# Weights of w_down's last row loaded into TensorE ahead of the wait for the last transfer

## The chip, the core and the metric

The kernel runs on one core of a Trainium2 chip. The core has a matrix engine (TensorE, PE in the profile; its weight loads are listed as PEld), VectorE (DVE), ScalarE (ACT), GpSimd (POOL) and SyncE (SP). Each works through its own list of instructions, in order, and they wait for each other on semaphores. Transfers between device memory and on-chip memory (SBUF) run on 16 DMA engines, fed from queues; PSUM is the memory into which TensorE accumulates.

The metric is the device time of one execution in microseconds (us), as the median of several runs. Before the change it is 656.65 us in 3 runs (656.56 to 656.92).

## The reference

One decoding step of a transformer layer for one token: attention over a cache of 65,536 positions, then a gated feed-forward layer, each with a layer norm ahead and the input added behind.

```python
x = A_x                                          # 1 x 512, bfloat16
h = x + attention(layernorm(x), k_cache, v_cache, wq, wo)   # 32 query heads on 8 cached heads, head size 128
g = layernorm(h) @ w_gate                        # 512 x 1792
u = layernorm(h) @ w_up                          # 512 x 1792
h2 = h + (sigmoid(g) * u) @ w_down               # 1792 x 512
```

The two caches are 8 x 65536 x 128 bfloat16 each, 128 MB apiece; with the weights the kernel reads 282.33 MB.

## The kernel before, in words

The kernel is written out instruction by instruction, with no scheduler. `op` and `dma` append an instruction to one engine's list with the names that it waits for; `emit` turns the names into semaphore waits. A wait for several names stands ahead of its instruction, and everything behind it on that engine waits too. Loops over the cached heads stand in the lists of TensorE and VectorE.

All loads go through SyncE's queue, in one order written by hand: wq, then the K and V caches head by head into a ring in SBUF (`ring`), wo in two pieces, w_gate, w_up, and last w_down. w_down is read as 128 partitions x 14 rows of 512 (row `r` of partition `p` is row 14p + r of the matrix), and it comes in four pieces by rows, `WD_SPLIT`: 0 to 7, 8 to 10, 11 and 12, and 13 alone. Each piece has a semaphore of its own (`wd0` to `wd3`). The last piece, one row of 128 KB, is the last load of the kernel.

Per block of the K cache, VectorE transposes pieces (L531) and TensorE multiplies them by the query (L443, `mm_at`). There, one weight load serves four matmuls: `kept=True` makes a matmul without a load of its own (`ldweights=False`), which takes the weights that are in the array. V is multiplied by the transposed probabilities on the same line.

The tail, after the last V piece:
- the head's output goes through wo (L640, L650), the second layer norm follows (L400 to L414), and `hc`, the centred input, is ready;
- w_gate and w_up are multiplied by `hc` (L847), 448 columns in each of four column groups of the array, and L852 brings the residual into the bank `YB` of PSUM, where the output is collected;
- VectorE and ScalarE make the gated product `hh` (L859) and VectorE transposes it into `hhT` (L863), in two halves of seven rows (`HH`);
- for each of the 14 rows, four matmuls (L869) add `hhT`'s column times a quarter of w_down's row into `YB`. Quarter `g` works in column group `g` of the array (`tile_position=(0, 32*g)`), so that the four can run side by side. The weights are columns of `hhT`: 32 of them for even `g`, of which the last gives the row of the output that is read later, and one for odd `g`. The moving operand is 128 columns of w_down's row. The first matmul of each piece waits for that piece, the first of each half for `hhT`;
- the very last matmul (`r` = 13, `g` = 3) raises `y`. VectorE (L873) and ScalarE (L874) copy the two halves of the output from PSUM into `y_sb`, and two DMAs write them (L877).

`zcol` is a column of 128 zeros in SBUF, set once by GpSimd at the start.

Of the kernel before, what the change touches and what calls it, by code (L numbers as in the profile page):

```python
# [35 lines left out]
class Prog:  # L36
# [14 lines left out]
    def op(self, eng, fn, deps=(), name=None, to=None, times=1):  # L51
        assert name is None or name not in self.where, name
        self.ops[eng].append(dict(fn=fn, deps=[d for d in deps if d], name=name, dma=None, to=to, times=times, part=self.part.get(eng)))
        if name:
            self.where[name] = (eng, len(self.ops[eng]) - 1)
# [168 lines left out]
def bass_sequential_preLN__gqa_block_cached__glu_gated_glu__decode_kernel(  # L224
# [15 lines left out]
    NF = FF // 128  # L240
# [6 lines left out]
    with ExitStack() as es:  # L247
        def sb(name, shape, dt):
            return es.enter_context(nc.sbuf_tensor(name, shape, dt))
# [23 lines left out]
        zcol = sb("zcol", [128, 1], bf16)  # L273
# [29 lines left out]
        hhT = sb("hhT", [128, 32 + FG], bf16)  # L303
# [11 lines left out]
        def ps(bank, c0, c1, p0=0, p1=128):  # L315
            return PS[p0:p1, bank * 512 + c0: bank * 512 + c1]
# [5 lines left out]
        op, dma = P.op, P.dma  # L322
# [95 lines left out]
        n = 128 // XR  # L418
# [209 lines left out]
        YT, STB, GB, UB, YB, OT = 0, MISC, 2, 3, 5, (1, 1)  # L628
# [167 lines left out]
        for i in range(HKV + 1):  # L796
            loop, last = 0 < i < HKV, i == HKV
# [43 lines left out]
        wd_v = ring[:, AT["wd"] * CH:AT["wd"] * CH + NF * D].rearrange("p (r n) -> p r n", r=NF)  # L841
        for i, (nm, bank) in enumerate((("wg", GB), ("wu", UB))):
            at = W_AT[nm]
            for kt in range(4):
                for c in range(4):
# [3 lines left out]
                        rhs=ring[:, at + kt * FF + c * FG: at + kt * FF + (c + 1) * FG],  # L849
                        start=(kt == 0), stop=(kt == 3), tile_position=(0, 32 * c)),  # L850
# [6 lines left out]
        HH = ((0, 7), (7, NF))  # L857
        for i, (r0, r1) in enumerate(HH):
            op("dve", lambda e, r0=r0, r1=r1: e.tensor_tensor(  # L859
                hh[:, 32 * r0:32 * r1].rearrange("p (r q) -> p r q", q=32),  # L860
                ps(UB, 0, FG).rearrange("p (q r) -> p r q", r=NF)[:, r0:r1, :],
                sg2[:, :].rearrange("p (q r) -> p r q", r=NF)[:, r0:r1, :], ALU.mult), ["gu1", "sg2"], f"hh{i}")
            op("dve", lambda e, r0=r0, r1=r1: e.transpose(hhT[:, 32 + 32 * r0:32 + 32 * r1], hh[:, 32 * r0:32 * r1]), [f"hh{i}"], f"hhT{i}")  # L863
        for i, (r0, r1) in enumerate(WD_SPLIT):
            for r in range(r0, r1):
                for g in range(4):
                    last = r == NF - 1 and g == 3
                    m, c = (1, 32 * r + 32) if g % 2 else (32, 32 * r + 1)
                    op("pe", lambda e, r=r, g=g, m=m, c=c: e.matmul(  # L869
                        ps(YB, 0, 128, 32 * g, 32 * g + m), lhsT=hhT[:, c:c + m], rhs=wd_v[:, r, g * 128:(g + 1) * 128],  # L870
                        start=False, stop=(r == NF - 1), tile_position=(0, 32 * g), skip_group_check=True),
                       ((["hhTz", f"wd{i}"] if r == r0 else []) + [f"hhT{j}" for j, (h0, _) in enumerate(HH) if r == h0]) if g == 0 else (), "y" if last else None)
        op("dve", lambda e: e.tensor_copy(y_sb[0:33, :], ps(YB, 0, 128, 0, 33)), ["y"], "ysb0")  # L873
        op("act", lambda e: e.activation(y_sb[64:97, :], ps(YB, 0, 128, 64, 97), AF.Copy), ["y"], "ysb1")  # L874
        for i, eng in enumerate(("sp", "act")):
# [32 lines left out]
```

## Time and profile before

One execution was recorded by the profiler. Its span, from the first to the last instruction, is 655.2 us; the page gives no other time of that execution, and the median of the timed runs is 656.65 us.

| What | Before |
|---|---|
| median of 3 runs | 656.65 us |
| span of the profiled execution | 655.2 us |
| TensorE busy, matmuls | 398.7 us (61%), 2317 instructions |
| TensorE busy, weight loads | 66.8 us (10%), 1549 instructions |
| VectorE busy | 350.3 us (53%) |
| ScalarE busy | 43.1 us (7%) |
| read from device memory | 282.33 MB, 431 GB/s over the span |
| share of the span that the load queue's packets fill | 99.6% |

How to read such a profile: an engine's busy time is the union of its instructions' times, and it says nothing by itself about what sets the end. The chain of waits does: it goes back from the last instruction, at each step to what released it. Groups of instructions stand in one line each, with the line of the kernel, the engine, the operation, what it writes and reads, the shapes and the count, then the busy time in us, the mean of one in ns, the idle time of the engine just before them, and what ended it. "128\*32 128x128" at a matmul is a weight matrix of 128 rows and 32 columns, with 128 rows and 128 columns streamed through it. The ends of matmuls are modelled, and matmuls overlap each other, so the sum of their durations is more than the busy time. The granted clock is the share of TensorE's full clock in a stretch.

### The profile page before, as it was taken

The numbers are of one execution on the slowest core, as the hardware profiler recorded it, in microseconds if no ns is written. First come the engines' busy times: TensorE is split into PE (matmuls) and PEld (weight loads), VectorE is DVE, ScalarE is ACT, GpSimd is POOL, SyncE is SP. The second block draws the span as 40 slices with busy tenths as digits, with TensorE's granted clock in tenths as the row PEclk, the third lists the DMA queues.
The fourth block names the chain that finished last, engine by engine and source line by source line (L and its number), as shares of the span: only waits on it lengthen the run. The fifth ranks groups of instructions, "written<-read, shape, count | busy, mean of one in ns | idle before, by whom it ended". The sixth has DMA issues, their size and how long they took to land.

```text
span 655.2 us, 6177 instructions
## 1 busy us (share of the span) xinstructions
PE 398.7 (61%) x2317; PEld 66.8 (10%) x1549; DVE 350.3 (53%) x428; ACT 43.1 (7%) x114; POOL 3.7 (1%) x19
## 2 busy tenths in 40 slices
PE   2778672937548293674828467393845739285466
PEld 1100010110101000010100101010010101001122
DVE  3398853819266290935719184481917548092202
ACT  1100200020000200002000200002000020001001
POOL 1000000000000000000000000000000000000000
PEclk9799695977959687785978769595796958778656
DMA  9999999999999999999999999999999999999998
GB/s 396 436 436 460 436 396 448 448 448 408 424 448 448 444 392 444 448 448 420 412 448 448 448 408 424 448 448 440 392 448 448 448 412 420 448 448 444 412 404 356
DMA packets 6376, 282.33 MB, mean 431 GB/s; under 512 B 744, under 2 KB 872, under 8 KB 1256
## 3 DMA queue, kind: packets, MB, share of 16 engines
q1 hardware_dynamic: 6340, 282.33, 99.6%
q10 hardware_dynamic: 36, 0.00, 0.0%
HBM read 282.33 MB, written 0.00 MB: 431 GB/s over the span
## 4 chain that ended last, share of the span: by engine, by line
DMA 66%; DVE 30%; PE 2%; issue 1%; SPq 0%; PEldq 0%
DMA ring<-in_A_k_cache_dram 58%; DVE ktw L531 30%; DMA ring<-in_B_w_up_dram 4%; DMA ring<-in_A_v_cache_dram 4%; PE PS L443 2%; PE PS L869 0%; PE PS L847 0%; DVE hh L859 0%; DVE hhT L863 0%; SPq L368 0%; SPq L339 0%; DVE y_sb L873 0%; PEldq L171 0%
## 5 line engine op out<-in xcount | busy, mean ns | idle before, releaser
L531 DVE STREAM_TRANSPOSE ktw<-ring 128x1024 f32<-128x1024 f32 x256 | 291.6, 1209 | 164.6 <-DMA ring<-in_A_k_cache_dram 164.5
L443 PE MATMUL PS<-ktw 128*128 128x512 bf16 x1024 | 276.7, 419 | 162.7 <-DVE ktw L531 155.0
L443 PE MATMUL PS<-ring,PT_sb 128*32 x1024 | 85.7, 422 | 54.7 <-issue 46.3
L443 PEld LDWEIGHTS PS<-ktw 128*128 x256 | 26.3, 103 | 401.1 <-issue 233.3
L618 ACT ACTIVATE po_sb<-PS,rl 128x512 bf16<-128x512 f32 x8 | 5.5, 687 | 523.4 <-PE PS L443 523.4
L443 PEld LDWEIGHTS PS<-ring,PT_sb 128*32 x1024 | 20.7, 116 | 117.7 <-issue 116.4
L566 DVE TENSOR_REDUCE gmj<-PS 1x4 f32<-1x128 f32 x8 | 2.2, 279 | 53.9 <-PE PS L564 53.9
L538 DVE TENSOR_REDUCE M_sb<-PS 128x1 f32<-128x512 f32 x32 | 19.9, 683 | 19.3 <-PE PS L443 19.3
L577 ACT ACTIVATE P_sb<-PS,negmax 128x512 bf16<-128x512 f32 x32 | 21.5, 685 | 0.3
L587 DVE STREAM_TRANSPOSE PT_sb<-P_sb 128x512 bf16<-128x512 bf16 x32 | 19.9, 675 | 1.7 <-ACT P_sb L577 1.7
L443 PE MATMUL PS<-ktw,xz 128*8 x32 | 9.7, 476 | 6.0 <-DMA ktw<-in_A_wq_dram 6.0
L634 DVE TENSOR_TENSOR Lw<-O,blk_of 128x896 bf16<-128x896 bf16 (+1 forms) x2 | 1.4, 682 | 16.0 <-ACT O L624 16.0
L489 DVE STREAM_TRANSPOSE qt<-qh 32x512 bf16<-32x512 bf16 x1 | 0.7, 699 | 14.8 <-ACT qh L486 14.8
L571 PE MATMUL PS<-one_f,gmrep 1*128 1x1 f32 x16 | 4.6, 357 | 5.0 <-DVE gmrep L568 5.0
L564 PE MATMUL PS<-identf,gm 128*1 128x128 f32 x16 | 4.5, 379 | 5.1 <-issue 2.9
L643 DVE CAST O<-PS 128x28 bf16<-128x28 f32 (+1 forms) x2 | 0.3, 174 | 12.7 <-PE PS L640 12.7
L577 ACT ACTIVATION_READ_ACCUMULATOR P_sb<-PS,negmax 128x1 f32 x32 | 6.5, 203 | 0.0
L621 PE MATMUL PS<-sel_bf,po_sb 128*128 128x4 bf16 x32 | 2.1, 170 | 6.3 <-ACT po_sb L618 6.3
L504 ACT ACTIVATE PS<-zcol 128x512 f32<-128x512 bf16 x8 | 5.0, 623 | 0.0
L573 ACT ACTIVATE negmax<-PS 128x1 f32<-128x1 f32 x8 | 1.4, 171 | 54.0 <-PE PS L571 54.0
L592 PE MATMUL PS<-L_sb,lsel 128*128 128x4 f32 x16 | 2.5, 229 | 3.8 <-DVE PT_sb L587 3.8
L571 PEld LDWEIGHTS PS<-one_f,gmrep 1*128 1x128 f32 x16 | 4.0, 306 | 8.8 <-DVE gmrep L568 8.8
(89 smaller groups left out, 65.4 us busy)
## 6 DMA issues: line engine op xcount, KB each, us to landing
ring<-in_A_k_cache_dram SPq DMA_DIRECT2D x4, 4096.0 KB, 34.8
ring<-in_A_v_cache_dram SPq DMA_DIRECT2D x1, 5120.0 KB, 30.0
ktw<-in_A_wq_dram SPq DMA_DIRECT2D x1, 4096.0 KB, 12.2
ktw<-in_A_wo_dram SPq DMA_DIRECT2D x1, 3584.0 KB, 18.3
ring<-in_A_v_cache_dram SPq DMA_DIRECT2D x1, 3072.0 KB, 36.8
ring<-in_B_w_gate_dram SPq DMA_DIRECT2D x1, 1792.0 KB, 23.4
ring<-in_B_w_up_dram SPq DMA_DIRECT2D x1, 1792.0 KB, 27.2
ring<-in_B_w_down_dram SPq DMA_DIRECT2D x1, 1024.0 KB, 29.2
```

The lines of the kernel that those rows point to most:

```text
L443: return e.add_instruction(mybir.InstMatmult(name=nc.get_next_instruction_name(), engine=mybir.EngineType.PE, ins=[rhs, lhsT], outs=[e.low ...
L504: op("act", lambda e: e.activation(ps(PO, 0, 512), bass.AP(tensor=zcol, offset=0, ap=[[1, 128], [0, 512]]), AF.Copy), ["zcol"] if h == 0 e ...
L531: op("dve", lambda e, d=dst, sr=src: e.transpose(d, sr), deps, f"T{b}.{c}", to="T")
L538: op("dve", lambda e, u=u: e.tensor_reduce(M_sb[:, u % 4:u % 4 + 1], ps(u % NS, 0, 512), AX.X, ALU.max), [f"S{b}.{NC - NR + k}"], f"mx{u}" ...
L564: op("pe", lambda e: e.matmul(ps(MISC, 0, 128, 0, 1), lhsT=gm[:, :], rhs=identf[:, :], start=True, stop=True), [f"gm{h}"], f"gmT{h}", to="Q")
L566: op("dve", lambda e: e.tensor_reduce(gmj[:, :], ps(MISC, 0, 128, 0, 1).rearrange("p (i a c) -> p a i c", a=4, c=NC), AX.XY, ALU.max), [f" ...
L571: op("pe", lambda e: e.matmul(ps(MISC, 128, 129), lhsT=gmrep[0:1, :], rhs=one_f[0:1, 0:1], start=True, stop=True), [f"gmrep{h}"], f"neg{h}")
L577: op("act", lambda e, b=b: e.activation(P_sb[:, (b % 4) * 512:(b % 4 + 1) * 512], ps(b % NS, 0, 512), AF.Exp, bias=negmax[:, k:k + 1], sca ...
L587: op("dve", lambda e, b=b: e.transpose(PT_sb[:, (b % 4) * 512:(b % 4 + 1) * 512], P_sb[:, (b % 4) * 512:(b % 4 + 1) * 512]), [f"E{b}"], f" ...
L592: op("pe", lambda e: e.matmul(ps(MISC, 132, 136), lhsT=lsel[:, :], rhs=L_sb[:, :], start=True, stop=True), [f"PT{NR * h + NR - 1}"], f"l{h ...
L618: op("act", lambda e: e.activation(po_sb[:, :], ps(PO, 0, 512), AF.Copy, scale=rl[:, :]), [f"PV{h}.{NR - 1}", f"rl{h}"], f"po{h}", to="po")
L621: op("pe", lambda e, t=t: e.matmul(ps(OX, 0, 4), lhsT=po_sb[:, t * 128:(t + 1) * 128], rhs=sel_bf[:, 8 * t:8 * t + 8:2], start=(t == 0), s ...
```

## The change

For the last row only (`r` = 13), four more matmuls stand ahead of the wait for the last piece. Each loads the weights that the last row's real matmul in its column group needs and multiplies them by the single zero column `zcol`, which adds zeros to the first column of that group's output. The four real matmuls come behind the wait and load no weights. All matmuls of w_down now go through the helper `down`, which builds the instruction itself with the same operands, tile sizes and positions as before. The waits, their order, the transfers and the work of the other engines are the same; TensorE's list has four matmuls more and as many weight loads as before.

```diff
+        def down(e, r, g, ahead, kept):
+
+            m, c = (1, 32 * r + 32) if g % 2 else (32, 32 * r + 1)
+            n = 1 if ahead else 128
+            rhs = zcol[:, :] if ahead else wd_v[:, r, g * 128:(g + 1) * 128]
+            more = dict(ldweights=False) if kept else {}
+            return e.add_instruction(mybir.InstMatmult(
+                name=nc.get_next_instruction_name(), engine=mybir.EngineType.PE, ins=[e.lower_ap(rhs), e.lower_ap(hhT[:, c:c + m])],
+                outs=[e.lower_ap(ps(YB, 0, n, 32 * g, 32 * g + m))], start_tensor_calc=False, stop_tensor_calc=r == NF - 1 and not ahead,
+                tile_size=(128, 32), tile_position=(0, 32 * g), bass_skip_group_check=True, **more))
+
         for i, (r0, r1) in enumerate(WD_SPLIT):
             for r in range(r0, r1):
+                end = r == NF - 1
+                if end:
+                    for g in range(4):
+                        op("pe", lambda e, r=r, g=g: down(e, r, g, True, False))
                 for g in range(4):
-                    last = r == NF - 1 and g == 3
-                    m, c = (1, 32 * r + 32) if g % 2 else (32, 32 * r + 1)
-                    op("pe", lambda e, r=r, g=g, m=m, c=c: e.matmul(
-                        ps(YB, 0, 128, 32 * g, 32 * g + m), lhsT=hhT[:, c:c + m], rhs=wd_v[:, r, g * 128:(g + 1) * 128],
-                        start=False, stop=(r == NF - 1), tile_position=(0, 32 * g), skip_group_check=True),
-                       ((["hhTz", f"wd{i}"] if r == r0 else []) + [f"hhT{j}" for j, (h0, _) in enumerate(HH) if r == h0]) if g == 0 else (), "y" if last else None)
+                    op("pe", lambda e, r=r, g=g, end=end: down(e, r, g, False, end),
+                       ((["hhTz", f"wd{i}"] if r == r0 else []) + [f"hhT{j}" for j, (h0, _) in enumerate(HH) if r == h0]) if g == 0 else (),
+                       "y" if end and g == 3 else None)
```

## The prediction, made before the changed kernel ran

> **What bounds the kernel now.** I read the page's head, its chain of waits and its queue table first, then the chain in the last microseconds, the waits, and the last group of matmuls by form.
>
> ```profile
> span 655.2 us, 6177 instructions
> ...
> q1 hardware_dynamic: 6340, 282.33, 99.6%
> ...
> DMA 66%; DVE 30%; PE 2%; issue 1%; SPq 0%; PEldq 0%
> ```
>
> The load queue's packets fill 99.6% of the span. The kernel is a stream of 282 MB, and TensorE (PE) matters only behind the last pieces of that stream. So the whole change is worth what it does between the landing of the last transfer and the last instruction. Stretches of time (us, busy by engine, granted clock, DMA share) show how small that piece is:
>
> ```profile
> 616.00:648.80 32.80, 20.58 (x183) 6.54 (x179) 2.57 (x14) 1.31 (x3) 0.55 (x1) 0.65 0.99 426
> 648.80:653.25 4.45, 3.92 (x70) 2.07 (x70) 2.22 (x5) 0.18 (x1) 0.00 (x0) 0.50 0.85 342
> 653.25:655.25 2.00, 0.31 (x10) 0.11 (x4) 0.28 (x1) 0.27 (x1) 0.00 (x0) 0.50 0.00 1
> ```
>
> The last 2.00 us have no loads left; TensorE runs there at half its clock (0.50). The timeline of that piece (start, duration, engine, what, what ended the idle time before):
>
> ```profile
> 652.96 0.14 PEld L869 LDWEIGHTS PS<-ring,hhT 128*32 128x32 bf16 x8
> ...
> 653.26 0.11 PEld L869 LDWEIGHTS PS<-ring,hhT 128*32 128x32 bf16 x4 [0.16 <-DMA ring<-in_B_w_down_dram]
> 653.62 0.27 ACT L874 ACTIVATE y_sb<-PS 33x128 bf16<-33x128 f32 x1 [4.63 <-PE PS L869]
> 653.62 0.28 DVE L873 CAST y_sb<-PS 33x128 bf16<-33x128 f32 x1 [1.19 <-PE PS L869]
> ```
>
> The eight weight loads at 652.96 are the two rows of the third piece of w_down. The four at 653.26 are the last row; they stood 0.16 us for the last transfer, and that wait is the only one here that ends on data. Behind it stand four loads, four matmuls, and then VectorE and ScalarE from 653.62. From the wait's end to 653.62 there are 0.36 us, and this is all the time that the change can touch. The casts, the output DMA and its landing follow unchanged.
>
> **The change part by part.**
>
> *Weight loads taken from behind the wait.* Before, each of the last four matmuls has its load behind the wait. After, the loads stand with four one-column matmuls ahead of it, and the last four matmuls take the kept weights. What this buys is not the loads' busy time, because a matmul starts together with its load. The last four matmuls by form (count, busy us, mean ns), with the loads of that stretch below them:
>
> ```profile
> L869 PE MATMUL PS<-ring,hhT 128*32 128x128 bf16 x2 | 0.3, 288 | 0.0
> L869 PE MATMUL PS<-ring,hhT 128*1 128x128 bf16 x2 | 0.3, 264 | 0.0
> ...
> L869 PEld LDWEIGHTS PS<-ring,hhT 128*32 128x32 bf16 x2 | 0.1, 103 | 0.2 <-DMA ring<-in_B_w_down_dram 0.2
> L869 PEld LDWEIGHTS PS<-ring,hhT 128*1 128x1 bf16 x2 | 0.1, 79 | 0.0
> ```
>
> With 32 weight columns the load takes 103 ns and the matmul 288. With one column it is 79 and 264. So 24 ns more load make 24 ns more matmul, and the rest of the load is either inside the matmul's own latency or in its 264. The trace can tell which, because the score matmuls (L443) already use kept weights. At the start of a block at 0.50 clock, one matmul with its load and two with kept weights each wait for VectorE:
>
> ```profile
> 303.40:304.20 0.80, 0.61 (x1) 0.10 (x1) 0.80 (x2) 0.00 (x0) 0.00 (x0) 0.50 2.83 1229
> 304.20:306.80 2.60, 1.17 (x2) 0.00 (x0) 2.60 (x4) 0.00 (x0) 0.00 (x0) 0.50 0.99 429
> ...
> L443 PE MATMUL PS<-ktw 128*128 128x512 bf16 x1 | 0.6, 606 | 7.7 <-DVE ktw L531 7.7
> ...
> L443 PE MATMUL PS<-ktw 128*128 128x512 bf16 x2 | 1.2, 584 | 1.1 <-DVE ktw L531 1.1
> ```
>
> A load of 105 ns ahead of it (0.10 in the first stretch) costs the matmul 606 − 584 = 22 ns, not 105. The kept matmul streams 512 columns in 584 ns. The last row's stream 128, and 384 columns fewer at half clock are 320 ns, if half clock is 1.2 columns a nanosecond; this is an estimate from the spacing of the rounds below (128 columns in 105 ns). That gives 264, which is what the one-column matmuls already take with their load. So the load of one column is free today and that of 32 columns costs 24 ns. Of the four, the third has 32 columns and ends last. Taken: 24 ns. Ends of the price: 0 (if the end hangs on the fourth, one-column matmul, which also carries the semaphore) and 0.11 us (all the loads' busy time).
>
> In a sentence by itself: the Trainium skill (TensorE: Matmul & The Clock Gate, section LDWEIGHTS) puts a load at columns ÷ 1.2 ns, so 27 ns for 32 columns and 1 for one; the trace's 103 − 79 = 24 agrees with the difference and not with the whole, and the sum by it would be 3 ns more.
>
> *Fewer instructions behind the wait.* Eight become four. The eight loads at 652.96 begin and end within 0.14 us, of which one load alone has 0.10, so eight follow each other within 0.04 and four within 0.02; I take 6 ns, between 0 and 0.02.
>
> *Four zero matmuls and their loads, ahead of the wait.* Their cover is the 0.16 us for which the weight loader idles. The rounds of the first seven rows show how fast a row goes:
>
> ```profile
> 651.72 0.94 PE L869 MATMUL PS<-ring,hhT 128*32 128x128 bf16 x28 [0.45 <-DVE hhT L863]
> ...
> L869 PE MATMUL PS<-ring,hhT 128*1 128x128 bf16 x4 | 0.4, 311 | 0.0
> ```
>
> 28 matmuls are seven rounds of four, side by side in the array. The last one of them takes about 311 ns, and so a round follows another after (0.94 − 0.31) ÷ 6 = 0.105 us. The third piece's two rounds begin at 652.96 and have streamed by about 653.17. The zeros then stream one column each. For a matmul of one column the nearest row is the wo projection, sixteen of them one after another:
>
> ```profile
> 644.84 0.69 PE L650 MATMUL PS<-O,ktw 128*128 128x1 bf16 x16 [0.26 <-DVE O L643]
> ```
>
> 0.69 less one latency of about 0.17 is 0.52 ÷ 15 = 35 ns each, one behind another and at the full clock; half clock doubles that at most, to 70. Side by side the four need one such step, one behind another four. So the array is free again between 653.21 and 653.45, and I take 653.24, since the rows above run side by side. The wait ends at 653.26, so the zeros cost nothing, with a margin of some 0.02 to 0.05 us. If the cover is gone (the last transfer landing with the one before), the price is the same 0.04 to 0.28 us less what the loads save. The PSUM column into which they add receives zeros; no other engine waits on them, and no wait or DMA is added or moved.
>
> *Sum, against the profiled span.* 655.2 − 0.024 − 0.006 = 655.17. The median of the runs, 656.65, is 1.45 above the span (start and end, which the trace does not hold, and the spread of the runs, 656.56 to 656.92). So 656.65 − 0.03 = 656.62. With the ends: 0.13 faster (0.11 + 0.02) to 0.19 slower (zeros done at 653.45), 656.52 to 656.84. I count as no change what stays within 0.2%, 1.31 us, about what a measurement of this kernel can tell.
>
> **The rivals.**
>
> *The zeros come late* (+0.2 us, 656.85). If a weight load could not run beside a matmul of the third piece, the four loads would begin when that piece's last matmul ends, at 653.36:
>
> ```profile
> 652.76 0.60 PE L869 MATMUL PS<-ring,hhT 128*1 128x128 bf16 x12
> ```
>
> Then 0.10 for the load, about 0.04 for a zero's step and 0.264 for the last matmul end at 653.76, against 653.26 + 0.29 = 653.55 now. Against it: a load (103) and a matmul (311) one after another would make a round of 0.41, and the rows above show 0.105, so loads do run beside matmuls of the same rows. For it: the margin is only some hundredths.
> Beside it stands the Trainium skill (TensorE: Matmul & The Clock Gate, section Part 3: Packing small matmuls, "What overlaps and what doesn't"), where loads overlap only with matmuls of other row groups, and all four here use the same rows; the rounds of this trace speak against that.
>
> *The change saves nothing* (656.65). The end is set by the fourth matmul, 264 ns before and after.
>
> *Slower: PE lacks its code* (+0.7 to +4.7 us). PE's list is four instructions longer, right before the last wait. If these push the end of the list over the edge of the piece of code that PE holds, PE stands between the third piece's rows and the last wait until the next piece is there. It decides as soon as that takes over the 0.16 us of cover. The trace shows no such load, so it is bounded by small transfers, from issue to landing, of the input x and of the output, where SyncE waits for the landing:
>
> ```profile
> xs<-in_A_x_dram ACTq DMA_DIRECT2D x1, 1.0 KB, 4.9
> ...
> SPq L221 <- DMA out_dram<-y_sb: 0.9, 1, 0.9
> ```
>
> 0.9 − 0.16 gives 657.4, 4.9 − 0.16 gives 661.4. A read is nearer to the first row, so I take 660. Against it: from 640 us on, the waits name data or an engine for every stretch in which the matmul side of PE stood; "issue" stands only at the weight loader:
>
> ```profile
> PEld PS L443 <- issue: 1.7, 2, 0.9
> ...
> PEld PS L847 <- issue: 0.9, 4, 0.2
> PEld PS L869 <- DMA ring<-in_B_w_down_dram: 0.9, 2, 0.7
> ...
> PEld PS L852 <- issue: 0.8, 1, 0.8
> ```
>
> There the loader stood while the matmuls ahead were still streaming. A list that arrives in time today for the 70 matmuls and 70 loads after 648.80 should do so for four more.
> The Trainium skill (Runtime: NRT & Kernel Launch, section Instruction fetch mechanics) says that code comes in blocks of 256 instructions and that crossing an edge is mostly hidden, a taken branch not; no run here shows either.
>
> *Faster by more than 0.2%.* All the time from the last wait's end to the two casts is 0.36 us, so no mechanism of the change reaches 1.31. Only the same edge of code, moved to the better side, could do it, by 1.3 us or more; nothing shows that it costs that today.
>
> **How the numbers follow.** The forecast (−0.03) has 0.70, the zeros late 0.06, nothing saved 0.07: all three within 0.2%, 0.83 together. PE without its code has 0.13, of which 0.02 would stay within the bound, so slower is 0.11 and within 0.85. The moved edge has 0.04, which is faster. The range takes the ends of the sum (656.52 to 656.84), the spread of the runs around them (0.09 down, 0.27 up) and some of the slower case's lower end: 656.2 to 657.5. What it leaves out is mostly the slower case and the faster one.
>
> **What would show it right or wrong.** In the profile after, the four weight loads stand before the wait, and the last four matmuls start some 0.04 us after the last landing with about 264 ns each, all four alike. The casts start 0.33 us after the last wait's end instead of 0.36. The zeros begin before that wait's end, and PE idles for the last transfer still, by less than 0.16 us. The forecast is wrong if the last matmuls take more than 288 ns, if the zeros end behind the last landing, or if PE has an idle stretch in its tail with no releaser.

## The result, and the profile after

The changed kernel takes 660.25 us (median of 5 runs, 660.11 to 660.30), the kernel before 656.65 (656.47 to 657.41). The ratio is 1.0052, with a 95% interval of 1.0041 to 1.0063: slower by 3.6 us, where the forecast was 0.03 us faster.

Only 0.6 us of that are in the span of the profile, and the spans of the changed kernel's five runs (655.4 to 655.8 us) come near to the 655.2 of before. The page of the changed kernel, head and queue table:

```profile
span 655.8 us, 6181 instructions
...
q1 hardware_dynamic: 6340, 282.33, 99.6%
```

So the kernel's own instructions take about as long as before, and the loss lies outside the span. The profiled execution of the changed kernel has 660.3 − 655.8 = 4.5 us there, and its five runs have 4.5 to 4.8. The prediction had 1.45 us for the kernel before, which is a median less the span of another execution. In the 25 runs of the kernel before that were taken beside the first experiments, each with its own span, it is 1.3 to 1.4.

The tail itself did what the prediction said. Its timeline (start, duration, engine, what, and the idle time before):

```profile
653.08 0.88 PE L870 MATMUL PS<-ring,hhT 128*32 128x128 bf16 x24
653.62 0.18 PEld L870 LDWEIGHTS PS<-zcol,hhT 128*1 128x1 bf16 x4
653.73 0.24 PE L870 MATMUL PS<-zcol,hhT 128*1 128x1 bf16 x4
653.85 0.27 PE L870 MATMUL PS<-ring,hhT 128*32 128x128 bf16 x4
654.17 0.27 ACT L886 ACTIVATE y_sb<-PS 33x128 bf16<-33x128 f32 x1 [4.39 <-PE PS L870]
654.17 0.28 DVE L885 CAST y_sb<-PS 33x128 bf16<-33x128 f32 x1 [1.14 <-PE PS L870]
```

The first line holds the last matmuls of the rows ahead. The loads and zeros start ahead of 653.85, where the last four matmuls begin with no load behind them; from there to the casts it is 0.32 us, against 0.36 before. The trace also records when the last piece landed: at 653.81, 0.04 us ahead of the last four matmuls, as in the kernel before (653.22 and 653.26). So the zeros do not hold them up. From that landing to VectorE's cast it is 0.359 us, against 0.395 before. The four matmuls by form (mean ns after the bar):

```profile
L870 PE MATMUL PS<-ring,hhT 128*32 128x128 bf16 x2 | 0.3, 265 | 0.0
L870 PE MATMUL PS<-ring,hhT 128*1 128x128 bf16 x2 | 0.3, 264 | 0.0
```

288 has become 265, and the 264 of the one-column groups stayed.

The loss shows only in a view that goes past the span. The queues from 656 to 660 us (each digit is a slice of 0.1 us; then packets, MB and the share of 16 engines' time):

```profile
DMA  0000000000000000000600000000000000000000
GB/s 0 0 0 0 0 0 0 0 0 0 0 0 0 0 0 0 0 0 0 164 0 0 0 0 0 0 0 0 0 0 0 0 0 0 0 0 0 0 0 0
DMA packets 1, 0.02 MB, mean 4 GB/s; under 512 B 0, under 2 KB 0, under 8 KB 0
...
q8 instruction: 1, 0.02, 1.7%
```

One packet of the kind "instruction", 16384 bytes, starts in the slice at 657.9, 2.1 us after the kernel's last instruction. Its share is 1.7% of 16 engines over 4 us, which is about 1.1 us on one engine. These 2.1 and 1.1 us and the usual 1.3 to 1.4 add up to the 4.5 outside the span; what passes in the 2.1 us, no view shows. The kernel before has nothing of that kind in its span or behind it. Its queues from 653 us to the end:

```profile
DMA packets 8, 0.00 MB, mean 0 GB/s; under 512 B 8, under 2 KB 8, under 8 KB 8
...
q1 hardware_dynamic: 4, 0.00, 0.0%
q10 hardware_dynamic: 4, 0.00, 0.0%
```

### The profile page after: what moved, and what is told of

It is laid out like the page before. It is cut to its first block, busy times and chain, and to the rows that moved or that the text cites. A ratio compares the mean times of both kernels' runs of the same rounds, so it can differ in the third digit from the quotient of the medians.

```text
span 655.8 us, 6181 instructions
## 1 busy us (share of the span) xinstructions
PE 398.0 (61%) x2321; PEld 66.8 (10%) x1549; DVE 350.1 (53%) x428; ACT 43.1 (7%) x114; POOL 3.7 (1%) x19
## 4 chain that ended last, share of the span: by engine, by line
DMA 66%; DVE 30%; PE 3%; issue 1%; SPq 0%; PEldq 0%
DMA ring<-in_A_k_cache_dram 58%; DVE ktw L531 29%; DMA ring<-in_B_w_up_dram 4%; DMA ring<-in_A_v_cache_dram 4%; PE PS L443 2%; PE PS L870 0%; PE PS L847 0%; DVE hh L859 0%; DVE hhT L863 0%; SPq L368 0%; SPq L339 0%; DVE y_sb L885 0%; PEldq L171 0%
```

## The experiments

Two theories stood after that. C: PE's list, four instructions longer, pushes the instructions that close the program over the edge of a piece of code (the place where one piece ends and the next has to be there), and the next piece is fetched only when it is needed. T: the new form of the last row is itself what makes the end late. All times below are medians beside runs of the kernel before on the same chip.

**The same length, another place.** The kernel before, with four instructions that do nothing for the result (one load, three zero matmuls into an unused column) where PE waits for wq:

```diff
+        for i in range(3):
+            op("pe", lambda e, i=i: spare(e, i > 0), ["zcol"] if i == 0 else ())
```

`spare` multiplies `zcol` by itself; `kept`, its second argument, leaves out the load.

> The kernel before, with one more weight load and three one-column zero matmuls (four instructions) in PE's list near its head, where PE waits some 6 us for wq; the tail is as before. Theory C (PE's list has become four instructions too long; the instructions that close the program behind the kernel's last one pass the edge of a 16 KB piece of code, which is fetched only then): 660.2 us, span 655 to 656, and one instruction transfer of 16384 B some 2 us after the span's end. Theory T (the new form of the last row itself, zero matmuls and kept weights, makes the end of the program late): 656.6 us, no such transfer.

Measured: 660.10 us against 656.65, ratio 1.0053 (1.0036 to 1.0070), span 655.3. Its queues from 656 to 660 us:

```profile
DMA  0000000000000080000000000000000000000000
...
q8 instruction: 1, 0.02, 2.1%
```

The whole loss is there, and the transfer too, in the slice at 657.4, with a tail that is the old one. Theory T is refuted.

**The change, the old length.** The changed kernel, with w_up's rows in reverse order so that its first four matmuls keep w_gate's last weights:

```diff
+            kts = (3, 2, 1, 0) if i else (0, 1, 2, 3)
+            for k, kt in enumerate(kts):
...
+    more=dict(ldweights=False) if i and k == 0 else {}
```

> The changed kernel, with four weight loads saved elsewhere: w_up's rows are taken in the order 3, 2, 1, 0, and its first four matmuls keep the weights of w_gate's last four, which are the same. PE's list is then as long as before. Theory C: 656.6 us (0.03 to 0.1 below the kernel before), no instruction transfer after the span. Theory T: 660.2 us.

Measured: 656.58 us, ratio 0.9999 (0.9989 to 1.0008). From 656 to 660 us there is no transfer of any kind:

```profile
DMA packets 0, 0.00 MB, mean 0 GB/s; under 512 B 0, under 2 KB 0, under 8 KB 0
```

So the loss hangs on the length of PE's list and not on what the four instructions do.

**Another engine.** The kernel before with four memsets more on VectorE:

```diff
+        for i in range(4):
+            op("dve", lambda e, i=i: e.memset(scr[:, 40 + i:41 + i], 0.0))
```

> The kernel before, with four more one-column memsets in VectorE's list near its head, where it waits for x. Theory C, which ties the loss to PE's list of 483 instructions: 656.6 us, no instruction transfer after the span. A wider theory, that any longer program loses it: 660.2 us.

Measured: 656.66 us, ratio 1.000 (0.999 to 1.001). The time is as theory C has it, but the expectation of no transfer was wrong. The queues from 654 to 656 us (slices of 0.05 us):

```profile
DMA  0000090000000000000000000000000000000000
...
q8 instruction: 1, 0.02, 3.9%
```

A transfer of the same size starts in the slice at 654.25, 0.9 us before the span's end at 655.1, when the loads are over and the output is being written. It takes 3.9% of 16 x 2 us, 1.25 us, and costs nothing there. That the edge belongs to each engine's own list fits this, but the trace doesn't name the engine that asked, here or above: that the late transfer is PE's code rests on the runs in which only PE's list was changed. Why this one came so much earlier than PE's stays open.

**Where the edge lies.** Two more instructions (zeros and kept weights for the two 32-column groups alone) and three more (one load and two zero matmuls near the head of the kernel before):

```diff
-                    for g in range(4):
+                    for g in (0, 2):
...
-                    op("pe", lambda e, r=r, g=g, end=end: down(e, r, g, False, end),
+                    op("pe", lambda e, r=r, g=g, end=end: down(e, r, g, False, end and g % 2 == 0),
```

> The changed kernel, with the zero matmuls and kept weights for the two 32-column groups alone; the one-column groups load behind the wait as before. PE's list is two instructions longer than before instead of four. Theory C: 656.6 if the edge lies at three or four more, 660.2 if it lies at one or two more, and nothing between. Theory T: about half the loss, 658.4 us, if it goes by the count of zero or kept matmuls.

> The kernel before, with one weight load and two zero matmuls more near the head of PE's list: three instructions more. Theory C is a threshold between two more (656.6 us was not changed by more than the runs' spread) and four more (660.1): either 660.1 with an instruction transfer some 2 us after the span, or 656.6 with none; nothing between. If the loss grew with each instruction, it would be some 3 us x 3/4.

Two more: 657.02 us, ratio 1.0005 (0.9996 to 1.0015), and no instruction transfer; the total can't be told from no change. The time outside the span can: it is 1.5 to 1.7 us in all ten runs, against 1.3 to 1.4 in the 25 runs of the kernel before beside them and in the ten of the changed kernel in the old length. So some 0.3 us are lost behind the last instruction here already, where theory C had nothing between its two outcomes. The profile shows no transfer for it, and its cause is open.

In the tail of this kernel, the last matmuls begin at 653.16 and the casts at 653.43, 0.27 us:

```profile
653.16 0.23 PE L870 MATMUL PS<-ring,hhT 128*32 128x128 bf16 x4
653.16 0.08 PEld L870 LDWEIGHTS PS<-ring,hhT 128*1 128x1 bf16 x2
653.43 0.27 ACT L886 ACTIVATE y_sb<-PS 33x128 bf16<-33x128 f32 x1 [4.35 <-PE PS L870]
```

That stretch had the full clock (1.00), and so it is compared with the old tail at the full clock, in the kernel with four more at the head (653.39 to 653.69, 0.30). Counted from the recorded landing of the last piece to VectorE's cast, the old tail takes 337 ns there, this kernel 317, and the changed kernel in the old length, also at the full clock and with all four groups' weights kept, 308. So the 32-column groups bring 20 ns of the gain and the one-column groups 9.

Three more: 658.23 us, ratio 1.0023 (1.0008 to 1.0039), and neither of the two outcomes expected. The ten runs lie between 656.69 and 660.40: three up to 656.85, two at 657.2 to 657.4, and five from 659.1 up. At the edge itself the same program falls on either side, or between, by the run. The instruction transfer was there in the profiled run, after the span. Outside the span, four of the ten runs have the 1.6 to 1.7 us of two more, and the others 2.2 to 5.0. This is read as a transfer that sometimes comes in time; no short run of this kernel was profiled, and what decides it was not found.

**Far over the edge.** The changed kernel with 20 and with 56 instructions more at the head, to see whether the transfer moves with the edge:

```diff
+        for i in range(19):      # 55 in the other
+            op("pe", lambda e, i=i: spare(e, i > 0), ["zcol"] if i == 0 else ())
```

> The changed kernel with twenty instructions more near the head of PE's list (one weight load, nineteen zero matmuls), where PE waits for wq. Theory C1 (the missing piece of code is asked for when PE gets to its edge, and that edge moves forward through the closing instructions by as many as are added): the transfer starts earlier than the 2.2 us after the span that it has in the changed kernel, by 0.3 to 1 us, and the time is as much less: 659.2 to 660. Theory C2 (the request comes at a fixed point of the end, wherever the edge is): 660.2 again.

> The changed kernel with fifty-six instructions more near the head of PE's list. Theory C1: the edge now lies in or before the last matmuls instead of in the closing instructions, so the transfer starts before the output is written, near or ahead of 654 us, and runs beside the last work: 656.6 us, although the list is the longest of all; if the edge lies in the tail's matmuls and nothing fetches ahead, PE stands for 1 to 3 us inside the span instead (658 to 660, span 657 to 658). Theory C2: 660.2 us.

Measured: 657.76 us (1.0017, 1.0007 to 1.0026) and 658.03 (1.0020, 1.0011 to 1.0030), below the changed kernel with a longer list. Both theories on the place were wrong. The transfer did not come some tenths of a microsecond earlier, but early in the stream: at 101 us with 20 more, and at 94 us with 56 more. The kernel with 20 more, its queues from 100 to 103 us:

```profile
q1 hardware_dynamic: 16, 1.05, 81.7%
q8 instruction: 1, 0.02, 1.9%
```

1.9% of 16 x 3 us is 0.91 us on one DMA engine, beside the K and V loads. The 1.2 us that are lost now lie inside the span (656.5). The end of the stream shows how, in busy time by engine, clock, DMA share and GB/s; first the kernel before, then the one with 20 more:

```profile
652.00:653.00 1.00, 1.00 (x45) 0.77 (x40) 0.41 (x1) 0.00 (x0) 0.00 (x0) 0.50 0.62 221
653.00:654.00 1.00, 0.56 (x16) 0.21 (x12) 0.28 (x1) 0.27 (x1) 0.00 (x0) 0.50 0.00 0
```

```profile
652.00:653.00 1.00, 0.60 (x2) 0.30 (x2) 0.97 (x3) 0.00 (x0) 0.00 (x0) 0.50 0.70 256
653.00:654.00 1.00, 0.95 (x38) 0.88 (x42) 0.73 (x2) 0.00 (x0) 0.00 (x0) 0.50 0.07 26
```

Before, the loads end within the slice from 652. With 20 more, a share of 0.07 goes on through the next microsecond: 1/16 is 0.0625, so one DMA engine of the 16 is still working off its part, and the last pieces of w_down wait for it.

That this began with the code is in the trace's record of landings, sixteen for each load. In the kernel before, the last of the sixteen lands 0.08 to 0.16 us behind the fifteenth in every load. With 20 more it is up to 0.2 us in the loads that land by 89 us, and 1.3 to 1.4 in every later one, from 110 us to the last piece. One part stays late from the code transfer to the end. The trace doesn't name the DMA engines, so that it is the one that carried the code is the plain reading and not shown; nor is it shown why the 0.91 us became 1.3.

**The prefetch hint.** PE's list ends in a branch back that is never taken, with a prefetch hint at the list's start. The changed kernel without both, and with six instructions more at the head, so that its list is longer than that of the changed kernel:

```diff
-HINTED = ("pe", "dve", "act")
+HINTED = ("dve", "act")
...
+        for i in range(5):
+            op("pe", lambda e, i=i: spare(e, i > 0), ["zcol"] if i == 0 else ())
```

> The changed kernel without the never-taken backward branch and its prefetch hint in PE's list (four instructions of control less there), and six instructions more at the head, so that the list is one longer than in the changed kernel and over the edge too. Theory H (the hint holds back the fetch of the code that follows, so that it comes on demand): without it the next piece is fetched ahead, the transfer lies inside the span, and the time is 656.6 us or up to 1 us more for what the hint saved. If the hint has no part in it: 660.2 us with the transfer after the span.

> The changed kernel with two instructions more near the head of PE's list, the prefetch hint in place. Theory H (with the hint, the piece beyond the edge is not fetched until PE needs it, as long as the hinted branch itself lies before the edge): transfer some 2 us after the span, 660.2 us, span 655 to 656. If it was not the hint's absence but the greater length that moved the transfer to 101 us in the kernel without the hint (one instruction longer than the changed one): transfer near 101 us, 657.7 us, span 656.4.

> The changed kernel with ten instructions more near the head of PE's list, the hint in place. Between two more and twenty more, theory H has one switch, where the hinted branch passes the edge: either 660 us with the transfer after the span (perhaps a little earlier than 2.2 us behind it) or 657.7 us with it near 101 us. Nothing between.

Without the hint: 657.68 us (1.0015, 1.0005 to 1.0025), span 656.4, and the transfer stands in the queues from 100 to 103 us (1.9%), inside the span as theory H says; the time is 1.1 us above the kernel before, just over the 1 us that H allowed. With the hint and two instructions more than the change: 660.29 in two runs (1.0054, 1.0036 to 1.0072), span 655.7, and the transfer after the span:

```profile
DMA  0000000000000000600000000000000000000000
...
q8 instruction: 1, 0.02, 1.7%
```

So at about the same length, the hint keeps the code from being fetched at 101 us. The lengths are matched only to an instruction or so. The expected text calls the list without the hint one longer than that of the change. Six instructions come and, by the same text, four go, which makes it two longer; of the four, the trace records three. So a switch to the early fetch at exactly three more is not excluded. With the hint and ten more: 657.74 (1.0015, 1.0005 to 1.0026), span 656.4, the transfer at 101 us again. Between two and ten more there is a switch back to the early fetch. That it is where the hinted branch itself passes the edge was what H supposed; the runs show the switch, not its reason.

**The version that fits, once more.**

> The changed kernel in the old length of PE's list once more, in more rounds. The trace puts the last wait's end to the casts 0.03 us shorter than before, so 656.57 against 656.60 or so: a ratio of 0.9999, which the runs can't tell from 1. A ratio below 0.998 would say that the order of w_up's rows, or the zeros, bring more than the trace shows; one above 1.002 that they cost something.

Measured: 656.53 us against 656.59, ratio 0.9997 (0.9988 to 1.0006). It is 3.7 us below the changed kernel and can't be told from the kernel before.

## Why the prediction was wrong

The step that failed is in the rival on PE's code, in its own words: "A list that arrives in time today for the 70 matmuls and 70 loads after 648.80 should do so for four more." The runs showed that it does not. A list of that length plus three falls on either side by the run, and plus four one more piece of 16384 bytes is fetched, 2.1 us after the kernel's last instruction; the program then ends 3.6 us later. The likeliest case took no term for code, and the case that came true had 0.13.

The rival's place was wrong too. It had PE standing between the third piece's rows and the last wait, so the span would have grown, and it read the tail's waits for such a stop. The missing piece holds up something after the kernel's last instruction. That these are PE's closing instructions fits every run, but no view shows which instruction waits for the piece. So the waits inside the span could not show how near the edge was, and the 1.45 us outside the span, taken over into the sum as a constant, was the term that changed: to 4.5. That the rival's 660 came near 660.25 is chance. Its ends were taken from the landing of an input and of an output; the price measured is that of a piece that comes behind the last instruction, 3.45 to 3.7 us by the medians of three kernels.

The steps on the tail, by the terms of the sum:
- weight loads behind the wait, 24 ns: right. The 32-column matmuls went from 288 to 265 ns, the one-column ones kept their 264, and the kernel with zeros for the 32-column groups alone has 20 of the 29 ns that the full clock shows;
- fewer instructions behind the wait, 6 ns: the other 9 ns fit this. Both together, from the last landing to VectorE's cast, were 36 ns at half clock (395 to 359), against 30 in the sum;
- the zeros beside the third piece's rows: right that they begin ahead of the last landing and cost nothing. A zero took 208 to 211 ns by the groups of the trace, where the sum had a step of 35 to 70, so their records end at 653.97, behind the landing at 653.81. The prediction had named this as a sign of being wrong; but the last matmuls still start 0.04 us after the landing. The rival in which loads can't run beside matmuls is refuted: in the profile after, the zeros' loads begin at 653.62, while matmuls of the rows ahead run until 653.96;
- "nothing saved" falls by the same rows, though its sum can't be told from the forecast's by the time.

Had the list kept its length, the forecast of 656.62 would have met the 656.53 to 656.58 measured, within what the runs can tell; they can't tell it from no change either, so only the traces show the gain.

## What to carry to other kernels

Instructions that cost nothing where they stand can make an engine's list too long for the code that is there in time: here four more on PE cost 3.6 us at the end of the program. Try the same number of instructions at another place in the list, and the change at the old length. When a time moves and the span does not, look at the queues behind the span before looking for a cause in the kernel. And where one load serves two groups of matmuls, as with w_gate's last and w_up's first weights, keeping it pays for instructions elsewhere.

## What the hardware showed that was not expected

One piece of 16384 bytes of code had three prices here, by when it was fetched: 3.45 to 3.7 us behind the kernel's last instruction, 1.1 to 1.5 us at about 100 us in a stream that fills all 16 DMA engines, although the transfer takes one engine only 0.9 us, and nothing at 654.25 us, between the end of the loads and the end of the program, in the kernel with more instructions on VectorE. Between the first two, the prefetch hint decides in lists a few instructions over the edge; from ten more on, the early fetch comes in spite of the hint. In the early case one of the sixteen parts of each load is late from then to the end of the stream, by 0.9 to 1.4 us in the four kernels that show it.
